# First keys loaded from ScalarE, five weight tiles from GpSimd, mask and coarse values in shared tile shapes

## The chip, the cores and the metric

The kernel runs on one core of one Trainium2 chip. Its time is the device time of one execution in microseconds (us). Besides the matmul engine TensorE (PE) it uses VectorE (DVE), ScalarE (ACT), GpSimd (POOL) and SyncE (SP), which before the change issues every transfer.

## What is computed

Local plus coarse attention over 2 batches, 8 heads, 576 positions and 64 channels, and then two expert layers, one behind the other, on 1152 tokens of 512 channels (2048 hidden):

```python
q_d, k_d, v_d = means of q, k, v over groups of 4 positions            # 144 coarse positions
out_up = repeat(softmax(q_d @ k_d.T / 8) @ v_d, 4)                      # coarse attention
scores = where(abs(i - j) < 4, q @ k.T / 8, -1e9)                       # local attention
attn = out_up + softmax(scores) @ v
x = attn.transpose(0, 2, 1, 3).reshape(1152, 512)
h = x @ w_in                                                            # first expert
x = ((a0 + a1 h + a2 h^2 + a3 h^3) / (1 + |b0||h| + |b1| h^2 + 1e-6)) @ w_out
h = x @ w_in2                                                           # second expert
out = (h * tanh(softplus(h))) @ w_out2
```

The weights are float64 in memory and are taken as pairs of 32-bit words.

## The kernel before

**Attention** is cut into 18 units of 128 query rows of a pair of heads: 16 that take four windows of one pair of heads, and two mixed ones that take the last window of all four pairs. A unit loads its queries (`qload`, L643) and the values of its windows (`vload`, L658), and goes through these steps on TensorE: `pe_a` turns the queries by transposes (L546); `pe_b` writes the band mask into the score bank by one matmul of the doubled identity `eye2` with `mask` (L702), adds the local scores (L709, 64 x 32 tiles) and the coarse scores (L717); `pe_d` turns the normalized weights (L786, L791); `pe_e` makes the coarse values (L816: for each half of the coarse positions and each head one product, 64 output channels) and the local values (L826). Between these steps VectorE and ScalarE do the softmax, GpSimd the normalization (L770, L775) and, for each pair of heads, the sums of values (L615, L619) that the coarse values read. `od_c` (L839) copies the coarse values out on ScalarE, and the results go as a high and a low half to `xh` and `xl`. Keys come once for each pair of heads and batch (`prep`, L554 and L558) and are turned on TensorE too.

**Experts.** The 32 weight tiles of 1 MB are loaded into two `raw` buffers (L983, L988), joined to f32 by ScalarE and VectorE (L1000 to L1031) and split into a high and a low half. The first expert's products are L1144 (in) and L1277 (out), the second's L1514 and, by a Strassen-like scheme of seven products, L1458 (in), and L1279 (out).

**The order** of every engine is made by a planner when the program is built (`Plan.run`): it takes each step's engines, estimated cost and priority and, engine by engine, starts the ready step with the lowest priority number. `UOFF` moves the priorities of the 18 units, `GOFF` those of the first weight tiles, `LOFF` those of the query loads; `SECOND`, `CLEAD` and `SUMS` are further numbers of this kind. Where the planner finds TensorE without a step in the first stretch, it writes a warm-up matmul into the program (L527, on the zero tile `blank`, into a spare bank). At run time each engine goes through its list in order, each instruction waiting for its operands alone; a transfer of SyncE waits besides for the eighth one before it.

Of the kernel before, what the change touches and what calls it, by code (L numbers as in the profile page):

```python
# [12 lines left out]
BF16 = mybir.dt.bfloat16  # L13
# [3 lines left out]
AF = mybir.ActivationFunctionType  # L17
ALU = mybir.AluOpType
AX = mybir.AxisListType

NEG = -1.0e9
# [15 lines left out]
SUMS = 5  # L37
# [3 lines left out]
UOFF = [-3.0, 0.0, 0.0, 3.0, 4.5, 3.0, 3.0, -1.5, 6.0, 0.0, 0.0, -4.5, -4.5, 4.5, 6.0, 4.5, -1.5, -1.5]  # L41
GOFF = [0.0, 0.0, 0.0, 0.0, -4.0, -4.0, -10.0, -6.0, 2.0, -4.0, 10.0, 12.0]
# [37 lines left out]
class Plan:  # L80
# [33 lines left out]
    def run(self, names):  # L114
# [3 lines left out]
        landed, moved = [0.0] * QUEUED, 0.0  # L118
# [75 lines left out]
        while True:  # L194
            for e in names:
# [3 lines left out]
                while ready[e]:  # L199
# [14 lines left out]
                    if e == "pool" or e == "dve" and t.port:  # L214

                        begin = max(now, port[0])
                        port[0] = begin + t.engs[e]
                    end = until[e] = begin + t.engs[e] * (2 if e == "pe" and now < COLD else 1)
                    there = end + LAT[e]
                    if t.dma:  # L220
                        end = begin
# [51 lines left out]
def kernel(  # L273
# [34 lines left out]
    eye2 = const.tile([128, 128], BF16, name="eye2")  # L308
    mask = const.tile([128, 11, WK], BF16, name="mask")
    band = const.tile([64, 92], BF16, name="band")  # L310
# [140 lines left out]
    def bands():  # L451
        nc.gpsimd.affine_select(
            out=band, in_=band, compare_op=ALU.is_ge, fill=NEG, base=-8, pattern=[[1, 92]], channel_multiplier=-1,
        )
        nc.gpsimd.affine_select(
            out=band, in_=band, compare_op=ALU.is_ge, fill=NEG, base=14, pattern=[[-1, 92]], channel_multiplier=1,
        )

    def masks(kind, w, n):
        for b in range(2):  # L460
            h = slice(HB * b, HB * b + HB)
# [10 lines left out]
    def eyes():  # L472
        for h in range(2):
            nc.vector.tensor_copy(out=eye2[:64, 64 * h:64 * h + 64], in_=ident[:64, :64])
# [11 lines left out]
    def under():  # L486
        nc.vector.memset(eye2[64:], 0.0)
        nc.vector.memset(mask[64:], 0.0)

    t_m = add({"dve": 0.1}, lambda: nc.vector.memset(band, 0.0), -1900)  # L490
    t_un = add({"dve": 0.4}, under, -880)
    t_cd = add({"dve": 0.6}, zeros, -1000)
    t_bn = add({"pool": 0.5}, bands, -900, after=[t_m])
    t_mk = [
        add({"dve": 0.2 + 0.05 * len(ws)}, lambda x=(i, ws): [masks(x[0], *w) for w in x[1]], (-890, MKP, MKP)[i], after=[t_bn])
# [42 lines left out]
    kv_done, unit_pe = {}, {}  # L538
# [9 lines left out]
    def prep(bb, p, prio, slots, start):  # L548
        kn = Buf(kn_s + (wide_s["kn"] if start else []))

        def load():
            src = k[bb, 2 * p:2 * p + 2]
            if start:
                nc.sync.dma_start(  # L554
# [8 lines left out]
        ld = add({"sp": 0.65}, load, prio - KOFF, take=[kn], chain="ld", dma=[(0.65, 1.59 if start else 1.84)])  # L563
# [65 lines left out]
    def unit(u, slots, start):  # L629
# [33 lines left out]
        vl = add({"sp": 1.0}, vload, prio + VOFF, take=[vw], chain="vw", dma=[(0.45, 0.11)] * 8 if mixed else [(0.45, 0.33)] * 4)  # L663
# [35 lines left out]
        def pe_b():  # L699

            hs = [slice(0, 64), slice(64, 128)]
            nc.tensor.matmul(  # L702
                sc.v[:, :nw * WK], eye2, mask[:, m0:m0 + nw].rearrange("p w x -> p (w x)"), start=True, stop=False,
            )
# [18 lines left out]
            {"pe": 1.6 if mixed else 0.86}, pe_b, prio,  # L723
            after=tq + [kv_done[p] for p in pairs] + [t_i16, t_un, t_mk[kind]],
# [83 lines left out]

        def pe_e():

            hs = [slice(0, 64), slice(64, 128)]
            for i, p in enumerate(pairs):
                m = 16 * nw // len(pairs)
                for t in range(2):
                    for hh, h in enumerate(hs):
                        nc.tensor.matmul(  # L816
                            po.v[h, m * i:m * i + m], vd[p][:, t, hh, :], pT.v[:72, 256 + 128 * t + 64 * hh + m * i:256 + 128 * t + 64 * hh + m * i + m],
                            start=(t == 0), stop=(t == 1),
                        )
            for m in range(2):  # L820
                for b in range(2):
                    for hh in range(2):
                        for a in range(2):
                            h, r = hs[hh ^ a], slice(64 * a, 64 * a + WK)
                            c = 128 * m + h.start + HB * b
# [748 lines left out]
```

## Time and profile before

| | us |
|---|---|
| median of 3 runs | 482.04 (481.93 to 483.39) |
| the profiled execution | 482.31 |
| its span in the profile | 480.4 |
| TensorE busy | 469.4 |
| VectorE busy | 377.0 |
| ScalarE busy | 338.3 |
| GpSimd busy, nearly all in the first 125 us | 57.1 |

A row of the profile gives the line of the kernel, the engine, the operation and the tiles that it writes and reads. TensorE's matmuls overlap one another, so that what one costs in the queue is the distance of its start from the next one's, and not its recorded duration. An f32 product is recorded as two passes, an f32 transpose as one. In the first 125 us attention, the first expert's products and the warm-up matmuls stand mixed in TensorE's list; behind it there are the experts alone.

### The profile page before, as it was taken

Reading aid. Unit: us, or ns where it says so; the run is one execution under the profiler, and the core shown is the slowest. Engines: PE = TensorE matmul, PEld = TensorE weight load, DVE = VectorE, ACT = ScalarE, POOL = GpSimd, SP = SyncE. Lnnn points to the kernel's source line nnn. Section 1 sums busy time; section 2 is a strip of 40 time slices with the busy share of each in tenths; the row PEclk is TensorE's granted clock in tenths of the full one; section 3 lists DMA queues with packets and bytes.
Section 4 is the critical chain, followed back from the end, with each engine's and each line's share of the span. In section 5 each row is a group of like instructions: output and inputs, shape, how many; then the busy total and the mean of one; then the engine's idle time right before and its main releaser. Section 6 shows DMA issues by size and latency. Waiting matters only on the chain.

```text
span 480.4 us, 9823 instructions
## 1 busy us (share of the span) xinstructions
PE 469.4 (98%) x4052; PEld 429.1 (89%) x4052; DVE 377.0 (78%) x565; ACT 338.3 (70%) x529; POOL 57.1 (12%) x80
## 2 busy tenths in 40 slices
PE   8998999999999999999999999999999999999996
PEld 4667888889999999999999999898989898989885
DVE  6677999899899968997998999988596669524342
ACT  5678898786889799998879797578666446422320
POOL 2644434563000000000000000000000000000000
PEclk9999999999999999999999999999999999999999
DMA  9878887611522312343022022134304220000103
GB/s 170 196 178 198 243 200 188 166 37 35 176 89 88 123 54 89 96 125 131 0 89 88 1 88 89 39 111 146 143 15 162 87 89 1 1 0 0 67 0 132
DMA packets 45981, 47.18 MB, mean 98 GB/s; under 512 B 30576, under 2 KB 31344, under 8 KB 45936
## 3 DMA queue, kind: packets, MB, share of 16 engines
q1 hardware_dynamic: 45936, 46.54, 33.7%
q8 instruction: 32, 0.52, 0.5%
q14 instruction: 13, 0.11, 0.1%
HBM read 44.17 MB, written 2.36 MB: 97 GB/s over the span
## 4 chain that ended last, share of the span: by engine, by line
PE 73%; DVE 13%; DMA 8%; ACT 3%; SPq 2%; issue 1%; ACTq 0%
PE psum L1279 19%; PE psum L1144 18%; PE psum L1277 15%; PE psum L1458 11%; PE psum L1514 5%; DMA att<-in_q_dram 3%; DMA raw<-in_moe_w_in_dram 3%; DVE wt L1014 1%; PE psum L826 1%; DMA att<-in_v_dram 1%; DVE xl L1300 1%; PE psum L546 1%; SPq L643 1%; DVE wrk L1318 1%; DVE wo L1031 1%
## 5 line engine op out<-in xcount | busy, mean ns | idle before, releaser
L1144 PE MATMUL psum<-xh,wi 128*128 128x384 f32 (+1 forms) x336 | 83.4, 319 | 0.2 <-DVE wrk L1173 0.2
L1277 PE MATMUL psum<-gg,wo 128*128 128x384 f32 (+1 forms) x480 | 76.3, 313 | 0.0
L1277 PEld LDWEIGHTS psum<-gg,wo 128*128 128x128 f32 x480 | 72.8, 189 | 0.4 <-issue 0.2
L1144 PEld LDWEIGHTS psum<-xh,wi 128*128 128x128 f32 x336 | 59.1, 189 | 1.4 <-issue 0.9
L1144 PE MATMUL psum<-xl,wi 128*128 128x384 f32 (+1 forms) x168 | 52.4, 312 | 0.0
L1279 PE MATMUL psum<-wo,gg 128*128 128x512 f32 x216 | 51.7, 391 | 0.0
L1279 PE MATMUL psum<-wo,late_g 128*128 128x512 f32 x216 | 51.3, 391 | 0.0
L1279 PEld LDWEIGHTS psum<-wo,late_g 128*128 128x128 f32 x216 | 40.4, 188 | 8.0
L1279 PEld LDWEIGHTS psum<-wo,gg 128*128 128x128 f32 x216 | 40.4, 188 | 7.9
L1014 DVE SCALAR_TENSOR_TENSOR wt<-wt,raw 128x1024 int32<-128x1024 int32 x32 | 40.0, 1252 | 6.8 <-ACT wt L1000 6.5
L1000 ACT ACTIVATE wt<-raw 128x1024 f32<-128x1024 f32 x32 | 36.5, 1140 | 10.9 <-DVE wo L1031 4.8
L1007 ACT ACTIVATE raw<-raw 128x1024 int32<-128x1024 uint16 x32 | 36.7, 1147 | 5.1 <-DMA raw<-in_moe_w_out_dram 3.4
L1514 PE MATMUL psum<-xh,wi 128*128 128x384 f32 x128 | 34.5, 335 | 0.0
L1144 PEld LDWEIGHTS psum<-xl,wi 128*128 128x128 f32 x168 | 31.8, 189 | 0.0
L1390 DVE TENSOR_TENSOR part<-psum,part 128x512 f32<-128x512 f32 x27 | 17.8, 687 | 13.7 <-PE psum L1279 13.7
L1144 PE MATMUL psum<-xh,late_r 128*128 128x384 f32 x96 | 25.5, 334 | 0.0
L527 PE MATMUL psum<-blank 128*128 128x480 bf16 x86 | 22.9, 390 | 1.2 <-DVE band L490 1.2
L1031 DVE TENSOR_TENSOR wo<-wt,wo 128x1024 fp32r<-128x1024 f32 x14 | 17.1, 1219 | 8.7 <-ACT wo L1026 8.7
L1026 ACT ACTIVATE wo<-wt 128x1024 fp32r<-128x1024 f32 x11 | 11.7, 1062 | 17.1 <-DVE wt L1020 7.7
L1514 PEld LDWEIGHTS psum<-xh,wi 128*128 128x128 f32 x128 | 23.3, 188 | 0.2
L1164 ACT ACTIVATE wrk<-psum 128x768 f32<-128x768 f32 (+1 forms) x27 | 19.8, 734 | 5.1 <-PE psum L1144 4.8
L1088 ACT ACT_TABLE_LOAD x17 | 21.8, 1283 | 0.3
(165 smaller groups left out, 1043.5 us busy)
## 6 DMA issues: line engine op xcount, KB each, us to landing
raw<-in_moe_w_in_dram SPq DMA_DIRECT2D x16, 1024.0 KB, 6.0
raw<-in_moe_w_out_dram SPq DMA_DIRECT2D x16, 1024.0 KB
att<-in_v_dram SPq DMA_DIRECT2D x64, 48.0 KB, 4.0
out_dram<-part SPq DMA_DIRECT2D x9, 256.0 KB, 2.1
att<-in_q_dram SPq DMA_DIRECT2D x16, 128.0 KB, 4.2
att<-in_k_dram SPq DMA_DIRECT2D x6, 288.0 KB, 4.5
att<-in_v_dram SPq DMA_DIRECT2D x6, 256.0 KB, 5.7
wrk<-in_k_dram SPq DMA_DIRECT2D x2, 288.0 KB
```

Of the source, the lines that this page charges most:

```text
L527: nc.tensor.matmul(view[:, :480], blank[:, :128], blank, start=True, stop=True)
L1000: nc.scalar.activation(out=t.v, in_=words(r)[:, :, 1].bitcast(F32), func=AF.Prelu if fold else AF.Identity, scale=2.0 ** -112, **({"alpha" ...
L1007: nc.scalar.activation(out=words(r)[:, :, 0], in_=r.v.bitcast(U16).rearrange("p (n four) -> p n four", four=4)[:, :, 1], func=AF.Copy, sca ...
L1014: nc.vector.scalar_tensor_tensor(out=ti, in0=ti, scalar=3, in1=words(r)[:, :, 0], op0=ALU.logical_shift_left, op1=ALU.bitwise_or)
L1031: ENG[e].tensor_tensor(out=w.v[:, 1], in0=s.v, in1=w.v[:, 0].bitcast(F32), op=ALU.subtract)
L1088: nc.scalar.preload_act_table_set(name)
L1144: nc.tensor.matmul(st.h.v[:, i, :T], w.v[:, ww, ks], xx[:, kk, c0:c0 + T], start=(nn == 0 and (st.big or i == 0)), stop=(nn == 3 * KD - 1 ...
L1164: nc.scalar.activation(out=vw(st.a), in_=H(), func=AF.Square)
L1277: nc.tensor.matmul(A(d)[:, :T], w.v[:, ww, lo + d * 128:lo + (d + 1) * 128], vw(gg)[:, i, :], start=start, stop=stop)
L1279: nc.tensor.matmul(A(d), vw(gg)[:, i, sl], w.v[:, ww, lo:lo + DM], start=start, stop=stop)
L1458: nc.tensor.matmul(dst.v[:, :TW], wv.v[:, ww, at:at + 128], x(h, kk), start=bool(take) and nn == 0, stop=nn == 5, skip_group_check=not take,)
L1514: nc.tensor.matmul(h.v[:, i, :TW], w.v[:, ww, at:at + 128], xx[:, kk, c0:c0 + TW], start=nn == 0, stop=nn == 3 * KD - 1)
```

## The change

- The keys of the second and third pair of heads are issued from ScalarE at its start; before, from SyncE.
- The first five weight tiles are issued from GpSimd, each placed behind a chosen unit's local values (`AFTER`); this is a place in the planned order, and no wait of the program.
- The mask is added by four matmuls on the 64 x 32 tiles of the local scores; `eye2`, `mask` and `band` hold both partition halves for it.
- The coarse values of both heads come from one full-width product for each half of the coarse positions, which also makes the two head pairings that nobody reads; `od_c` then picks the two useful blocks by two instructions.
- The planner's numbers change: `UOFF`, `GOFF`, `LOFF`, `SECOND`, `CLEAD`, `SUMS`, and the costs that it takes for `pe_b`, `pe_e`, `od_c` and the masks; its model of the transfers keeps a queue of eight for GpSimd apart.

```diff
-SECOND = 1.8
+SECOND = 1.2
-LEAD, CLEAD, LLEAD, OLAG = 38, 14, 40, 18
-PROL, PSTEP, VOFF, VROFF, LOFF, KOFF = -45, 2.5, 2, -1, 7, 9
+LEAD, CLEAD, LLEAD, OLAG = 38, 12, 40, 18
+PROL, PSTEP, VOFF, VROFF, LOFF, KOFF = -45, 2.5, 2, -1, 10, 9
-SUMS = 5
+SUMS = 0
+AFTER = [1, 3, 4, 5, 6]
+AHEAD = 2
-GOFF = [0.0, 0.0, 0.0, 0.0, -4.0, -4.0, -10.0, -6.0, 2.0, -4.0, 10.0, 12.0]
+GOFF = [0.0, 0.0, 0.0, 0.0, -4.0, -4.0, -20.0, -10.0, 8.0, 2.0, 0.0, 4.0]
...
     def masks(kind, w, n):
-        for b in range(2):
-            h = slice(HB * b, HB * b + HB)
+        for r0 in range(0, 128, HB):
+            b, h = r0 // HB % 2, slice(r0, r0 + HB)
...
+        ahead = start and 0 < p <= AHEAD
+
         def load():
             src = k[bb, 2 * p:2 * p + 2]
             if start:
-                nc.sync.dma_start(
+                (nc.scalar if ahead else nc.sync).dma_start(
...
-            nc.tensor.matmul(
-                sc.v[:, :nw * WK], eye2, mask[:, m0:m0 + nw].rearrange("p w x -> p (w x)"), start=True, stop=False,
-            )
+            for b in range(2):
+                for h in hs:
+                    r0 = h.start + HB * b
+                    nc.tensor.matmul(
+                        sc.v[r0:r0 + HB, :nw * WK], eye2[h, HB * b:HB * b + HB],
+                        mask[h, m0:m0 + nw].rearrange("p w x -> p (w x)"), start=True, stop=False, tile_position=(h.start, r0),
+                    )
...
-            {"pe": 1.6 if mixed else 0.86}, pe_b, prio,
+            {"pe": 1.52 if mixed else 0.78}, pe_b, prio,
...
                 for t in range(2):
-                    for hh, h in enumerate(hs):
-                        nc.tensor.matmul(
-                            po.v[h, m * i:m * i + m], vd[p][:, t, hh, :], pT.v[:72, 256 + 128 * t + 64 * hh + m * i:256 + 128 * t + 64 * hh + m * i + m],
-                            start=(t == 0), stop=(t == 1),
-                        )
+                    nc.tensor.matmul(
+                        po.v[:, 2 * m * i:2 * m * i + 2 * m], vd[p][:, t].rearrange("p h d -> p (h d)"),
+                        pT.v[:72, 256 + 128 * t:384 + 128 * t].rearrange("p (h x) -> p h x", h=2)[:, :, m * i:m * i + m],
+                        start=(t == 0), stop=(t == 1),
+                    )
...
-            {"pe": 1.75 if mixed else 0.98}, pe_e, prio, after=tp + [vl] + [vd_done[p] for p in pairs], take=[po, px, od, xt],
+            {"pe": 1.6 if mixed else 0.89}, pe_e, prio, after=tp + [vl] + [vd_done[p] for p in pairs], take=[po, px, od, xt],
...
         def od_c():
-            nc.scalar.activation(
-                out=od.v[:, :16 * nw], in_=po.v[:, :16 * nw], func=AF.Identity, scale=0.25
-            )
+            for hh in range(2):
+                h = slice(64 * hh, 64 * hh + 64)
+                nc.scalar.activation(
+                    out=od.v[h].rearrange("c (i x) -> c i x", x=m),
+                    in_=po.v[h, :128].rearrange("c (i h x) -> c i h x", h=2, x=m)[:, :, hh], func=AF.Identity, scale=0.25,
+                )
...
-        def load(g=g, r=r):
+        own = len(W) < len(AFTER)
+
+        def load(g=g, r=r, q=nc.gpsimd if own else nc.sync):
...
-        x = add({"sp": 0.5}, load, pr - LLEAD, take=[r], chain="wld", dma=[(0.5, 3.97)])
+        x = add({"pool" if own else "sp": 0.5}, load, pr - LLEAD, after=[v_loads[AFTER[len(W)]]] if own else [], take=[r],
+                chain="wld", dma=[(0.85 if own else 0.5, 3.97)])
```

TensorE's list holds 86 warm-up matmuls before and 112 now, 67 and 76 of them ahead of the first L1144; the matmuls of the experts are the same in number and size. SyncE's list at the program's start, before (L554 keys, L643 queries, L609 the values of a pair of heads, L658 the values of a unit's windows):

```order
L554 DMA att<-in_k_dram 96x2x384
L643 DMA att<-in_q_dram 128x4x64
L554 DMA att<-in_k_dram 96x2x384
L609 DMA att<-in_v_dram 64x2x512
L609 DMA att<-in_v_dram 8x2x512
L643 DMA att<-in_q_dram 128x4x64
L554 DMA wrk<-in_k_dram 96x2x384
L643 DMA att<-in_q_dram 128x4x64
L658 DMA att<-in_v_dram 48x4x64 x4
```

and now (the keys are L555, queries L645, values L611 and L660):

```order
L555 DMA att<-in_k_dram 96x2x384
L645 DMA att<-in_q_dram 128x4x64
L611 DMA att<-in_v_dram 64x2x512
L611 DMA att<-in_v_dram 8x2x512
L645 DMA att<-in_q_dram 128x4x64 x2
L660 DMA att<-in_v_dram 48x4x64 x4
```

Two of the three keys that stood in this list are gone from it; they now open ScalarE's list, ahead of its table load. GpSimd's list around the third unit, before (L615 and L619 sums of values, L870 the low half `xl`, L770 and L775 the normalization of a unit):

```order
L615 TENSOR_TENSOR wrk<-wrk 72x4x128
L619 TENSOR_TENSOR att<-wrk 72x2x2x64
L870 TENSOR_TENSOR xl<-att,xh 128x256
L770 TENSOR_TENSOR att<-att 128x4x48
L775 TENSOR_SCALAR att<-att 128x144
```

and now (L617, L621, L880, L776 and L781 in the same meaning, L995 the load of a weight tile):

```order
L617 TENSOR_TENSOR wrk<-wrk 72x4x128
L621 TENSOR_TENSOR att<-wrk 72x2x2x64
L995 DMA raw_74<-in_moe_w_in_dram 128x4x256
L617 TENSOR_TENSOR att<-att 72x4x128
L880 TENSOR_TENSOR xl<-att,xh 128x256
L776 TENSOR_TENSOR att<-att 128x4x48
L781 TENSOR_SCALAR att<-att 128x144
```

The first weight tile is issued here, and the normalization of the third unit now stands behind it and behind the fourth sum of values. TensorE's list at the first unit's scores and at its values, before:

```order
L702 LDWEIGHTS eye_62
L702 MATMUL psum<-mask,eye_62 128x192
L709 MATMUL psum<-att 32x48 x16
L717 MATMUL psum<-att 32x144 x4
...
L816 MATMUL psum<-att 64x64 x4
L826 MATMUL psum<-att 64x32 x16
```

and now (mask L707, local scores L715, coarse scores L723, coarse values L822, local values L833; the first two rows stand four times in a row):

```order
L707 LDWEIGHTS eye_62
L707 MATMUL psum<-mask,eye_62 32x192
...
L715 MATMUL psum<-att 32x48 x16
L723 MATMUL psum<-att 32x144 x4
...
L822 MATMUL psum<-att 128x128 x2
L833 MATMUL psum<-att 64x32 x16
```

The mask is cut into four tiles of 32 output rows, and four coarse products of 64 x 64 became two of 128 x 128; in the two mixed units 16 products of 64 x 16 became 8 of 128 x 32.

## Rows read from the trace of the kernel before

**Rows 1.** The page: busy us of each engine, share of the span, instructions.
```profile
PE 469.4 (98%) x4052; PEld 429.1 (89%) x4052; DVE 377.0 (78%) x565; ACT 338.3 (70%) x529; POOL 57.1 (12%) x80
```
**Rows 2.** Windows by stage: stretch and length, busy us by engine, clock, DMA share, GB/s.
```profile
0.00:33.00 33.00, 30.01 (x488) 18.46 (x489) 21.81 (x72) 21.22 (x56) 15.98 (x30) 1.00 0.90 194
...
125.00:260.00 135.00, 135.00 (x806) 135.00 (x805) 124.12 (x137) 119.39 (x137) 0.00 (x0) 1.00 0.27 90
260.00:310.00 50.00, 49.36 (x273) 47.39 (x272) 47.26 (x56) 38.78 (x47) 0.00 (x0) 1.00 0.12 43
```
**Rows 3.** Groups of the page (busy, mean ns), then TensorE's timeline (start, length).
```profile
L527 PE MATMUL psum<-blank 128*128 128x480 bf16 x86 | 22.9, 390 | 1.2 <-DVE band L490 1.2
...
29.39 1.78 PE L527 MATMUL psum<-blank 128*128 128x480 bf16 x8
31.01 0.38 PE L786 MATMUL psum<-ident,att 128*112 128x128 f32 x2
31.22 0.38 PE L791 MATMUL psum<-ident,att 128*72 128x128 f32 x2
```
**Rows 4.** TensorE's waits: for whom, us in total, times, longest.
```profile
PE psum L546 <- DMA att<-in_q_dram: 2.8, 3, 1.6
...
PE psum L816 <- POOL att L619: 1.1, 2, 0.7
PE psum L826 <- DMA att<-in_v_dram: 0.9, 2, 0.6
PE psum L1458 <- DVE wrk L1480: 0.6, 1, 0.6
```
**Rows 5.** TensorE's timeline at an unmixed unit, then at a mixed one.
```profile
34.48 0.28 PE L1144 MATMUL psum<-xh,wi 128*128 128x256 f32 x1
34.69 0.45 PE L816 MATMUL psum<-att 72*64 72x64 f32 x8
35.07 0.67 PE L826 MATMUL psum<-att 48*64 48x32 f32 x32
...
36.27 0.28 PE L1144 MATMUL psum<-xl,wi 128*128 128x256 f32 x1
36.39 0.28 PE L1144 MATMUL psum<-xh,wi 128*128 128x256 f32 x1
36.51 0.26 PE L702 MATMUL psum<-mask,eye 128*128 128x192 bf16 x1
36.70 0.54 PE L709 MATMUL psum<-att 64*32 64x48 f32 x32
...
64.77 1.11 PE L816 MATMUL psum<-att 72*64 72x16 f32 x32
65.81 0.67 PE L826 MATMUL psum<-att 48*64 48x32 f32 x32
```
**Rows 6.** Weight loads of 0 to 125 us by form: busy us, mean ns, idle before.
```profile
L1144 PEld LDWEIGHTS psum<-xh,wi 128*128 128x128 f32 x139 | 23.5, 190 | 1.4 <-issue 0.9 <-DVE wrk L1173 0.5
...
L816 PEld LDWEIGHTS psum<-att 72*64 72x64 f32 x192 | 7.1, 137 | 4.6 <-POOL att L619 1.6 <-issue 1.0 <-ACT att L801 0.6
...
L546 PEld LDWEIGHTS psum<-ident,att 128*128 128x128 f32 x36 | 4.2, 141 | 4.1 <-issue 1.8 <-DMA att<-in_q_dram 1.8
```
**Rows 7.** Chain that ended last (start, length), then SyncE's timeline.
```profile
17.15 2.02 SPq L983
19.27 6.06 DMA att<-in_q_dram
...
35.49 0.40 SPq L983 DMA_DIRECT2D raw<-in_moe_w_in_dram  x1
```
**Rows 8.** GpSimd's timeline: start, length, instruction, in brackets the idle time ahead of it.
```profile
28.20 1.31 POOL L615 TENSOR_TENSOR att<-att 72x512 f32<-72x512 f32 x1 [5.02 <-DMA att<-in_v_dram]
29.47 0.51 POOL L770 TENSOR_TENSOR att<-att 128x192 f32<-128x192 f32 x1
```
**Rows 9.** ScalarE's groups of 0 to 125 us: busy us, mean ns, idle before.
```profile
L839 ACT ACTIVATE att<-psum 128x64 f32<-128x64 f32 x18 | 4.0, 224 | 7.2 <-PE psum L826 7.0
```
**Rows 10.** SyncE's waits of 0 to 125 us: us in total, times, longest.
```profile
SPq L983 <- DVE wt L1014: 4.6, 1, 4.6
```

More of the change, by code (lines that the diff above doesn't have):

```diff
@@ L117, in run @@
         live, freed, port = {}, {}, [0.0]
-        landed, moved = [0.0] * QUEUED, 0.0
+        lanes, moved = {"sp": [0.0] * QUEUED, "pool": [0.0] * QUEUED}, 0.0
+        lanes["act"] = lanes["sp"]
         touched = {}
@@ L213, in run @@
                     begin = max(now, 0.65) if e == "sp" else now
-                    if e == "pool" or e == "dve" and t.port:
+                    if e == "pool" and not t.dma or e == "dve" and t.port:
                         begin = max(now, port[0])
@@ L220, in run @@
                     if t.dma:
-                        end = begin
+                        end, landed = max(begin, 0.65), lanes[e]
                         for issue, move in t.dma:
@@ L485 @@
     t_id = add({"pool": 1.1}, lambda: make_identity(nc, ident), -1000)
-    def under():
-        nc.vector.memset(eye2[64:], 0.0)
-        nc.vector.memset(mask[64:], 0.0)
     t_m = add({"dve": 0.1}, lambda: nc.vector.memset(band, 0.0), -1900)
-    t_un = add({"dve": 0.4}, under, -880)
     t_cd = add({"dve": 0.6}, zeros, -1000)
-    t_bn = add({"pool": 0.5}, bands, -900, after=[t_m])
+    t_bn = add({"pool": 1.0}, bands, -900, after=[t_m])
     t_mk = [
-        add({"dve": 0.2 + 0.05 * len(ws)}, lambda x=(i, ws): [masks(x[0], *w) for w in x[1]], (-890, MKP, MKP)[i], after=[t_bn])
+        add({"dve": 0.4 + 0.1 * len(ws)}, lambda x=(i, ws): [masks(x[0], *w) for w in x[1]], (-890, MKP, MKP)[i], after=[t_bn])
         for i, ws in enumerate((((0, 1), (1, 1), (2, 1), (3, 1)), ((4, 4),), ((8, 4),)))
@@ L561, in load @@
                 )
-        ld = add({"sp": 0.65}, load, prio - KOFF, take=[kn], chain="ld", dma=[(0.65, 1.59 if start else 1.84)])
+        ld = add({"act" if ahead else "sp": 0.65}, load, -2000 if ahead else prio - KOFF, take=[kn],
+                 chain=None if ahead else "ld", dma=[(0.65, 1.59 if start else 1.84)])
         copies = []
@@ L661, in vload @@
                     )
-        vl = add({"sp": 1.0}, vload, prio + VOFF, take=[vw], chain="vw", dma=[(0.45, 0.11)] * 8 if mixed else [(0.45, 0.33)] * 4)
+        vl = v_loads[len(v_loads)] = add({"sp": 1.0}, vload, prio + VOFF, take=[vw], chain="vw", dma=[(0.45, 0.11)] * 8 if mixed else [(0.45, 0.33)] * 4)
         def pe_a():
@@ L722, in unit @@
         tb = add(
-            {"pe": 1.6 if mixed else 0.86}, pe_b, prio,
-            after=tq + [kv_done[p] for p in pairs] + [t_i16, t_un, t_mk[kind]],
+            {"pe": 1.52 if mixed else 0.78}, pe_b, prio,
+            after=tq + [kv_done[p] for p in pairs] + [t_i16, t_mk[kind]],
             take=[sc, tm, s, pd],
@@ L807, in unit @@
         ]
+        m = 16 * nw // len(pairs)
         def pe_e():
@@ L838, in od_c @@
         def od_c():
-            nc.scalar.activation(
-                out=od.v[:, :16 * nw], in_=po.v[:, :16 * nw], func=AF.Identity, scale=0.25
-            )
-        to = add({"act": 0.11}, od_c, prio, after=[tf], use=[po, od])
+            for hh in range(2):
[3 more added lines that the diff above has]
+                    in_=po.v[h, :128].rearrange("c (i h x) -> c i h x", h=2, x=m)[:, :, hh], func=AF.Identity, scale=0.25,
+                )
+        to = add({"act": 0.21}, od_c, prio, after=[tf], use=[po, od])
         def xadd():
```

32 lines of the change are left out of this document (16 added, 16 removed).

## The prediction, written before the changed kernel ran

> **What bounds the kernel now.** I read the busy line first: TensorE is busy for 469.4 of 480.4 us, every other engine far less [rows 1]. The windows by stage say where the remainder lies: from 125 us to 260 us TensorE never stops, and around the change of experts it stands for 0.64 us in 50; the first 33 us hold 3 us of its idle time [rows 2]. The reader is to see a queue that is almost always full, so that the end moves by exactly what is put into that queue, taken out of it, or waited for in front of it. Some of what it holds is no work: the 86 warm-up matmuls on `blank` [rows 3]. Last I read TensorE's own waits [rows 4]: queries that have not landed (2.8 us in three waits), local values (0.9 us), the coarse values made by GpSimd (1.1 us), and 0.6 us at the first Strassen products.
>
> So I use a ledger: time = real matmuls + warm-up matmuls + waits + a head and a tail that the change leaves alone. It stands on one profiled execution of 482.31 us (span 480.4, 1.9 outside it), 0.27 us above the median of 482.04.
>
> **Warm-up matmuls.** They are written into the program by the planner, and run whether or not TensorE would have waited. The order has 86 before and 112 now: 67 and 76 of them ahead of the first expert matmul, 19 and 36 behind it. Eight in a row, from 29.39 to 31.01 us, take 1.62 us, so one is 0.20 us of queue [rows 3]. That adds 26 x 0.20 = **+5.2 us**. It costs nothing where it stands in place of a wait; the gain then shows in the term of the waits, which for the whole attention stage is at most 2.8 + 1.1 + 0.9 = 4.8 us [rows 4]. This bound is why I doubt a gain: the added filler is as large as all that waiting.
>
> **Mask in tile shapes, 18 units.** One full-array matmul of 192 columns becomes four on 64 x 32 tiles. Before, 0.19 us pass from the mask's start (36.51) to the first local score (36.70), although 256 columns in the full array take 0.12 us (36.27 to 36.39) [rows 5]. Some 0.10 us are therefore not the mask's columns but the change to tiles behind it. The same change shows where a full-array matmul is followed by the tiled coarse values: 0.21 us (34.48 to 34.69) in place of 0.12. The change now stands ahead of the mask instead of behind it. I take 0.02 us less each, **-0.4 us**. Bounds: the change of shape vanishes (18 x -0.10 = -1.8), or the two column tiles of a row half stream one after the other (another 192 columns, 0.08 by the 256-column row: +1.4). The Trainium skill ("TensorEngine Tiling (Array Packing)", Key Properties) says that a change of tiling mode drains TensorE; the rows agree, with 0.09 us, and by that rule the 0.10 us cannot be won by giving the mask its followers' shape, while a reading without it would book -1.8.
>
> **Coarse values in one shape.** Before, an unmixed unit has four products 72 x 64 with 64 columns, recorded as eight passes in 0.38 us (34.69 to 35.07), two column tiles side by side [rows 5]. Now two full-width products with 128 columns each compute all four head pairings, of which half are thrown away, in four passes. A full-array f32 pass with 128 columns takes 0.105 us (31.01 to 31.22 for two transposes) [rows 3]. Four are 0.42, and leaving for the 64 x 64 tiles of the local values costs 0.09 as above; entering from a full-array matmul saves 0.09. So 0.42 against 0.38: +0.04, and +0.13 where the work ahead is tiled, which I take for a third of the units: 16 x 0.07 = +1.1. In the two mixed units 16 products with 16 columns take 1.04 us (64.77 to 65.81); that is weight loading, 32 passes in pairs of 64 columns. Now there are 8 products, 16 passes, each with 128 weight columns. A load of 64 columns is recorded with 0.137 us, one of 128 with 0.190 (0.053 more per 64 columns, so 0.106 for 128), yet 0.141 for the transposes [rows 6]. At 0.106 they take 1.70, +0.66 each; at half, 0.85, -0.19 each. I take a value towards the upper row, since it is the one of plain products: 2 x 0.6 = +1.2. Together **+2.3 us**. Bounds: all passes at half (4 x 0.053 = 0.21 against 0.38, 16 x -0.17, with the mixed ones -3.1), or entry never saved and loads in full (16 x 0.13 + 2 x 0.75 = +3.6).
>
> **Loads.** Two keys leave SyncE for ScalarE and five weight tiles of 1 MB leave it for GpSimd. At 17.15 us SyncE spends 2.02 us on a weight issue, the query load behind it is issued at 19.27 and lands 6.06 us later, and TensorE waits for it [rows 7]. With the tile on another queue neither delay is in front of that query, and the query loads also come earlier in the order. I take 3.0 of the 3.7 us of waits for loads as gone: **-3.0 us**; bounds 0 and -3.7. ScalarE's two issues stand at its start, ahead of its table load, when TensorE runs warm-up matmuls; if that cover is gone they cost two issues, 0.8 us at the 0.40 us of the shortest issue in [rows 7].
>
> **GpSimd's queue.** No row of before shows a DMA issued there. An issue of the same tile costs SyncE 0.40 us, or 2.02 us when it is held up [rows 7]. Behind it in GpSimd's queue stand the sums of values, `xl`, and the normalization of the next unit, for which ScalarE, VectorE and then the transposes of TensorE wait. GpSimd is on the chain already: at 28.20 it had waited 5.02 us for a values load, with the normalization of a unit behind it [rows 8]. Five issues of about 1 us, most of it beside other work: **+0.6 us**, bounds -1.0 (that 5.02 us shortens) and +4.
>
> **Other work.** `od_c` becomes two ScalarE instructions of about 0.22 us [rows 9]: 18 x 0.22 = 4 us of ScalarE, beside TensorE, whose next products in the queue do not read that copy: 0 us, and 1 us if that cover is gone. Twelve more mask copies on VectorE and two selects on GpSimd lie ahead of the first scores, under warm-up matmuls: 0. In the second expert the order of Strassen sums, wide output products and first Strassen products changes: 36 wide output products now stand ahead of all Strassen products, where 0.6 us was waited [rows 4]. VectorE is busy for 47.26 of the 50 us there [rows 2], so I book 0 with bounds -0.6 and +2.
>
> **Sum.** 5.2 - 0.4 + 2.3 - 3.0 + 0.6 = +4.7 us. 482.31 + 4.7 = 487.0 against the profiled execution, **486.7** against the median, 1.0% slower.
>
> **Rivals.**
> *The cheap shapes win.* The full-width passes take half of what I say and the mask loses its change of shape: -3.1 - 1.8, and all waits go: 5.2 - 4.9 - 4.8 = -4.5, 477.5 us; with 3.0 of the waits gone 479.3. For it: a transpose's weight load of 128 columns is recorded with 0.141, not 0.190. Against it: transposes with 128 columns still pass at 0.105 us each. It decides if the coarse values take 0.25 us or less in an unmixed unit.
> *Nothing comes of it.* Coarse values at their old price, the mask half-way to its lower bound (-1.0), all load waits gone and GpSimd half-way to its own (-0.5): 5.2 - 1.0 - 3.7 - 0.5 = 0, 482 us.
> *The loads land no earlier.* All bytes move through the same engines; the tile still takes its share beside the query. Then the -3.0 falls away: 489.7. For it: in the first 33 us the engines are 0.90 busy [rows 2]. Against it: part of the delay was SyncE's own 2.02 us. The Trainium skill ("DMA: Bandwidth & Descriptors", Issuing engines are not separate DMA queues) says that DMAs started by any engine interleave on the same 16 engines and that issuing from several saves only the issue time; by that rule this rival would be the forecast, 489.7, and no run here has yet shown it.
> *GpSimd is held up.* SyncE once waited 4.6 us in front of a weight issue, until VectorE had joined the tile that held the buffer [rows 10]. If such a wait now stands in GpSimd's queue, a normalization waits behind it and TensorE with it: up to +4.6, 491.3 us.
>
> **How the numbers follow.** Forecast, 483.5 to 489: 0.45. Loads no earlier: 0.13. GpSimd held up: 0.15. Nothing: 0.14. Cheap shapes: 0.13. Three cases are slower: 0.73; 0.3% (1.4 us), about what a measurement of this kernel can tell from no change, leaves 0.14 for the same and 0.13 for faster. The range reaches down into the cheap shapes, 480.5, and up to the held GpSimd, 491.5, and leaves some 0.17 out.
>
> **What would show it.** The warm-up group at 112 instructions of 0.20 us in a row; an unmixed unit's coarse values near 0.42 us plus the change of shape, a mixed unit's near 1.7; the mask's start to the first local score near 0.09, with 0.21 in front of it; TensorE's waits for queries under 1 us. The forecast is wrong if the coarse values got cheaper, if the waits shrank by more than 4 us, or if TensorE waits for GpSimd's normalization by several us.

## The result, and the profile after

The changed kernel takes 486.74 us (486.17 to 488.83), 1.0104 times the kernel before (95% interval 1.0065 to 1.0143): 4.7 us slower, as forecast (486.7). Ratios here and below leave out the runs that took over 1.5% longer than the fastest of their kernel (one of twelve with five tiles from GpSimd, two of nine with mask and five tiles); medians count them. The profiled execution took 486.17 us, its span is 484.4 us. The page, with TensorE's busy time and matmuls, against [rows 1]:

```profile
PE 477.1 (99%) x4036; PEld 435.1 (90%) x4036; DVE 381.3 (79%) x576; ACT 343.7 (71%) x546; POOL 65.2 (13%) x87
...
L526 PE MATMUL psum<-blank 128*128 128x480 bf16 x112 | 29.6, 393 | 1.2 <-DVE band L490 1.2
```

TensorE is busy for 7.7 us more with 16 matmuls fewer; 6.7 us of this are recorded for the warm-up matmuls alone (22.9 before, [rows 3]). Windows by stage, columns as in [rows 2], first two of the kernel before, then the changed one:

```profile
33.00:48.00 15.00, 13.38 (x276) 11.20 (x278) 11.07 (x34) 12.92 (x32) 6.14 (x10) 1.00 0.71 167
48.00:125.00 77.00, 75.13 (x1394) 67.00 (x1393) 71.17 (x143) 61.51 (x147) 34.98 (x41) 1.00 0.61 156
```
```profile
0.00:33.00 33.00, 30.72 (x493) 18.79 (x493) 23.11 (x88) 21.12 (x59) 17.04 (x34) 1.00 0.82 179
33.00:48.00 15.00, 15.00 (x303) 11.78 (x305) 11.37 (x27) 12.29 (x34) 9.53 (x11) 1.00 1.03 228
48.00:125.00 77.00, 76.69 (x1316) 68.71 (x1309) 69.28 (x139) 64.72 (x155) 38.61 (x44) 1.00 0.48 130
125.00:260.00 135.00, 135.00 (x816) 135.00 (x815) 124.91 (x138) 119.57 (x138) 0.00 (x0) 1.00 0.28 95
260.00:310.00 50.00, 49.21 (x271) 47.13 (x270) 48.82 (x58) 40.28 (x47) 0.00 (x0) 1.00 0.18 63
```

In the first 125 us TensorE's idle time fell from 6.5 to 2.6 us, and from 33 to 48 us it no longer stands. Even so it has started 322 matmuls of the first expert by 125 us, and 352 before: 30 at 0.12 us [rows 5] are 3.6 of the 4.0 us between the two spans. Behind 125 us little changed (0.79 us stood around the change of experts, 0.64 before). So nearly all of the difference lies in the first 125 us. TensorE's waits, against [rows 4]:

```profile
PE psum L526 <- DVE band L490: 1.2, 1, 1.2
PE psum L545 <- ACT att L762: 0.8, 1, 0.8
...
PE psum L822 <- POOL att L621: 0.3, 1, 0.3
```

No wait for a load is left: of the 2.8 us for queries and 0.9 us for local values nothing, of the 1.1 us for the sums of GpSimd 0.3. TensorE's timeline, in the places of [rows 3, 5] (three unmixed units, then a mixed one, then a mask behind an expert matmul):

```profile
20.24 0.71 PE L822 MATMUL psum<-att 72*128 72x128 f32 x4
20.88 0.67 PE L833 MATMUL psum<-att 48*64 48x32 f32 x32
...
34.83 0.61 PE L822 MATMUL psum<-att 72*128 72x128 f32 x4
35.37 0.67 PE L833 MATMUL psum<-att 48*64 48x32 f32 x32
...
43.73 0.58 PE L526 MATMUL psum<-blank 128*128 128x480 bf16 x2
44.15 0.38 PE L792 MATMUL psum<-ident,att 128*112 128x128 f32 x2
...
44.58 1.78 PE L526 MATMUL psum<-blank 128*128 128x480 bf16 x8
46.20 0.61 PE L822 MATMUL psum<-att 72*128 72x128 f32 x4
46.74 0.67 PE L833 MATMUL psum<-att 48*64 48x32 f32 x32
47.34 0.26 PE L707 MATMUL psum<-mask,eye 64*32 64x192 bf16 x4
47.43 0.51 PE L715 MATMUL psum<-att 64*32 64x48 f32 x32
...
64.22 0.28 PE L1157 MATMUL psum<-xh,wi 128*128 128x256 f32 x1
64.34 1.87 PE L822 MATMUL psum<-att 72*128 72x32 f32 x16
66.14 0.67 PE L833 MATMUL psum<-att 48*64 48x32 f32 x32
...
67.46 0.29 PE L1157 MATMUL psum<-xh,wi 128*128 128x256 f32 x1
67.68 0.26 PE L707 MATMUL psum<-mask,eye 64*32 64x192 bf16 x4
```

Read by starts: the unmixed coarse values take 0.54 us behind full-array work (34.83 to 35.37; 0.38 before) and 0.64 behind the tiled coarse scores (20.24 to 20.88), the mixed ones 1.80 (64.34 to 66.14; 1.04 before), the mask 0.09 to its first local score (47.34 to 47.43; 0.19 before). Ten warm-up matmuls stand around the transposes, where [rows 5] has none. The first of the five issues on GpSimd, its timeline beside [rows 8]:

```profile
20.72 0.97 POOL L995 DMA_DIRECT2D raw<-in_moe_w_in_dram  x1
22.55 1.26 POOL L617 TENSOR_TENSOR att<-att 72x512 f32<-72x512 f32 x1 [0.86 <-DMA att<-in_v_dram]
```

An issue costs GpSimd 0.76 to 0.97 us and none waits for its buffer; GpSimd's 5.02 us in front of the sums became 0.86.

### The profile page after: what moved, and what is told of

Read it like the earlier page. It is cut to its first block, busy times and chain, and to the rows that moved or that the text cites. A ratio compares the mean times of both kernels' runs of the same rounds, so it can differ in the third digit from the quotient of the medians.

```text
span 484.4 us, 9858 instructions
## 1 busy us (share of the span) xinstructions
PE 477.1 (99%) x4036; PEld 435.1 (90%) x4036; DVE 381.3 (79%) x576; ACT 343.7 (71%) x546; POOL 65.2 (13%) x87
## 4 chain that ended last, share of the span: by engine, by line
PE 81%; DVE 11%; DMA 3%; ACT 2%; issue 1%; POOL 1%; SPq 0%; POOLq 0%; DVEq 0%
PE psum L1157 19%; PE psum L1292 18%; PE psum L1290 15%; PE psum L1471 11%; PE psum L1527 5%; PE psum L526 4%; PE psum L822 2%; PE psum L833 2%; DMA raw<-in_moe_w_in_dram 2%; PE psum L545 1%; DVE part L1380 1%; DVE xl L1313 1%; ACT att L589 1%; PE psum L723 1%; DVE wt L1026 1%; PE psum L715 1%
## 5 line engine op out<-in xcount | busy, mean ns | idle before, releaser
L526 PE MATMUL psum<-blank 128*128 128x480 bf16 x112 | 29.6, 393 | 1.2 <-DVE band L490 1.2
L1537 ACT ACTIVATE wrk<-psum 128x768 f32<-128x768 f32 x8 | 6.5, 814 | 24.5 <-PE psum L1527 24.5
```

What stands on the lines that cost most here:

```text
L526: nc.tensor.matmul(view[:, :480], blank[:, :128], blank, start=True, stop=True)
```

## The experiments

**How they add up.** Three groups of four kernels, each group on one chip, with runs of the kernel before between them (medians 481.1, 481.7 and 481.1 us). A kernel's median is compared within its group, the ratio across groups. Lines of an edited kernel are shifted by a few.

| kernel | us | ratio to before | 95% |
|---|---|---|---|
| changed, again | 487.02 | 1.0121 | 1.0097 to 1.0145 |
| changed, coarse values in old shapes | 483.64 | 1.0048 | 1.0030 to 1.0066 |
| changed, all loads from SyncE | 486.31 | 1.0118 | 1.0086 to 1.0151 |
| changed, last 36 warm-ups left out | 488.25 | 1.0141 | 1.0106 to 1.0177 |
| changed, 10 warm-ups left out | 486.19 | 1.0103 | 1.0079 to 1.0127 |
| changed order alone | 485.57 | 1.0088 | 1.0050 to 1.0127 |
| before, mask in tiles | 479.72 | 0.9965 | 0.9944 to 0.9986 |
| before, coarse values in new shape | 482.44 | 1.0009 | 0.9981 to 1.0037 |
| before, five tiles from GpSimd | 479.66 | 0.9961 | 0.9938 to 0.9983 |
| before, mask and five tiles | 478.78 | 0.9953 | 0.9923 to 0.9982 |
| the same, keys from ScalarE | 478.81 | 0.9979 | 0.9950 to 1.0009 |
| before, 5 more warm-ups | 480.32 | 0.9981 | 0.9961 to 1.0000 |

**The changed kernel again.**

> The changed kernel once more, unaltered, as the measure for the others of this group, which are all cut from it. Expected 486.7 us again, a ratio to the kernel before of 1.010 (1.0065 to 1.0143 so far).

487.02 us, 5.8 us above the kernel before by its ratio; it is the measure for the next three.

**Coarse values back in their old shapes**, with their one copy out, at their places in the changed order:

```diff
-                    nc.tensor.matmul(
-                        po.v[:, 2 * m * i:2 * m * i + 2 * m], vd[p][:, t].rearrange("p h d -> p (h d)"), ...
+                    for hh, h in enumerate(hs):
+                        nc.tensor.matmul(
+                            po.v[h, m * i:m * i + m], vd[p][:, t, hh, :], ...
```

> The changed kernel with the coarse values alone in their old shapes: for each head and half a product with 64 output channels, one copy out; every instruction stands at its place as before the edit. Ledger: the full-width products cost 16 x 0.06 us in unmixed units and 2 x 0.67 us in mixed ones by their starts in the two traces, so this version is 2.3 us faster than the changed kernel, 484.4 us (486.7 - 2.3). Rival, the shapes cost nothing because a later wait takes what they give: 486.7 us, and TensorE's waits in the attention stage grow by 2.3 us. Rival, full-width products are the cheaper ones: 487 us or more.

483.64 us, 3.4 less; the two intervals do not meet, so the new shape costs time here. TensorE's timeline of this version at an unmixed unit behind coarse scores and at a mixed unit:

```profile
19.71 0.45 PE L824 MATMUL psum<-att 72*64 72x64 f32 x8
20.10 0.67 PE L834 MATMUL psum<-att 48*64 48x32 f32 x32
...
63.32 0.28 PE L1155 MATMUL psum<-xh,wi 128*128 128x256 f32 x1
63.53 1.11 PE L824 MATMUL psum<-att 72*64 72x16 f32 x32
64.57 0.67 PE L834 MATMUL psum<-att 48*64 48x32 f32 x32
```

From the full-array matmul ahead to the local values it is 1.25 us (63.32 to 64.57), in the changed kernel 1.92 (64.22 to 66.14): 0.67 for one mixed unit. In 13 unmixed units the work ahead uses the full array, and they differ by 0.07 each (0.16 more for the coarse values, 0.09 less ahead of them). In three, coarse scores in tiles stand ahead; nothing is saved there, and they differ by 0.26 each (0.64 and 0.38). Together 2 x 0.67 + 13 x 0.07 + 3 x 0.26 = 3.0 of the 3.4 us; the rest is within the two intervals.

**All loads issued from SyncE again**, at their places in the changed order:

```diff
-                (nc.scalar if ahead else nc.sync).dma_start(
+                nc.sync.dma_start(
...
-        def load(g=g, r=r, q=nc.gpsimd if own else nc.sync):
+        def load(g=g, r=r, q=nc.sync):
```

> The changed kernel with the two keys and the five weight tiles issued from SyncE again, at the places in the planned order that they have in the changed kernel; TensorE, VectorE and the work of GpSimd keep their order. Theory that the other queues removed the waits for loads: TensorE's waits for queries and values come back, 3 to 4 us, and the time is 489.7 to 490.7 us. Rival, the planned order alone removed them, since all bytes move through the same 16 DMA engines: 486.7 us, with TensorE's waits as small as in the changed kernel (3.1 us in the listed rows). Third, the five issues on GpSimd cost it 0.76 to 0.97 us each and TensorE paid for it: 484 to 486 us.

486.31 us, no difference from 487.02. Its TensorE waits of the first 125 us:

```profile
...
PE psum L545 <- ACT att L762: 0.8, 1, 0.8
PE psum L545 <- ACT att L677: 0.4, 1, 0.4
```

No wait for queries or values, without the other queues. None of the seven profiles with the changed order has a wait for queries, whatever the queues; each of the four with the order before and all loads on SyncE has some (0.8 to 2.8 us). So in the changed kernel the planned order removed these waits, not the queues, and issuing from other engines was worth nothing that can be measured there (1.0118 against 1.0121). The Trainium skill ("DMA: Bandwidth & Descriptors", Issuing engines are not separate DMA queues) says that it saves only the time of the issue; this run agrees.

**The last 36 warm-up matmuls left out, then ten of them.** They are no part of the result. The first edit; the second has `if not 76 < len(warmed) <= 86`:

```diff
+        warmed.append(1)
+        if len(warmed) <= 76:
             nc.tensor.matmul(view[:, :480], blank[:, :128], blank, start=True, stop=True)
```

> The changed kernel without the last 36 of its 112 warm-up matmuls, those that stand behind the first expert matmul in TensorE's list; they are no part of the result. Ledger, each costs 0.20 us of a full queue: 36 x 0.20 = 7.2 us, 479.5 us. Rival, they stand in place of waits for work that is not ready: TensorE's waits grow by what they took, and the time stays at 486.7 us. Between the two the growth of the waits gives the share; with the clock of TensorE granted in full throughout in either case. If the granted clock falls below 1.00 in the first 125 us, a third cause is there and the time may rise above 486.7 us.

488.25 us: some 7.2 us of queue were taken out, and by the median none of it was gained. TensorE's timeline without the 36, and two windows (busy PE, PEld, DVE, ACT, POOL, then clock):

```profile
55.43 0.40 PE L796 MATMUL psum<-ident,att 128*112 128x128 f32 x2 [1.38 <-ACT att L593]
...
60.70 0.63 PE L1161 MATMUL psum<-xh,wi 128*128 128x256 f32 x2
61.13 0.41 PE L1161 MATMUL psum<-xl,wi 128*128 128x256 f32 x1
```
```profile
54.00:58.00 4.00, 2.62 (x52) 1.82 (x52) 3.25 (x7) 3.94 (x9) 2.11 (x3) 0.72 0.92 215
58.00:62.00 4.00, 4.00 (x47) 3.71 (x45) 3.56 (x7) 3.80 (x9) 0.00 (x0) 0.50 0.66 215
```

Where seven warm-up matmuls ran, TensorE now stands for 1.38 us, until ScalarE has made what the transposes read; then the granted clock falls to 0.50, the 1.2 GHz level, and the 256-column passes follow each other at 0.21 us (60.70 to 61.13 for two) in place of 0.12 [rows 5]. By the windows TensorE's idle time of the first 125 us is 6.9 us in place of 2.6, 4.3 more; the mean clock of this profile, 0.993 over 485 us, is 3.4 us of full clock that are missing. Together they are about what was taken out. So waits came back for more than half, and the clock took the rest: five of the six runs have a mean clock of 0.993 or less, and the sixth, at 1.00, took 485.19 us, 1.8 less than the changed kernel.

> The changed kernel without ten of its warm-up matmuls, those that run from 43.7 to 46.0 us, ahead of the waits that followed when all 36 later ones were left out; warm-up matmuls are no part of the result. If the ten are pure cost: 10 x 0.20 = 2.0 us less than the changed kernel, 485.0 us, 1.008 of the kernel before. If they stand in place of waits: TensorE waits there instead, 487.0 us, and if the standing is long enough the granted clock falls below 1.00 behind it and the time rises to 488 us or more.

486.19 us: 0.9 less by the ratios, between the two answers, and the interval meets that of the changed kernel. The clock held (0.998 or more in all six runs). TensorE's timeline without the ten, to be read against 43.73 to 47.43 of the changed kernel above:

```profile
43.57 0.38 PE L796 MATMUL psum<-ident,att 128*112 128x128 f32 x2
...
44.37 0.71 PE L826 MATMUL psum<-att 72*128 72x128 f32 x4 [0.20 <-DVE att L860]
...
46.05 0.26 PE L711 MATMUL psum<-mask,eye 64*32 64x192 bf16 x4 [0.30 <-ACT att L758]
```

The transposes start 0.58 us earlier, the coarse values 1.83, the mask only 1.29: the work behind the removed matmuls was not ready, and waits for VectorE (0.20) and ScalarE (0.30, and 0.8 a little later) stand in their place.

**The changed order alone**: coarse values and loads undone as above and the mask too, so that only the planner's numbers and costs (and the copies for the second half of the mask) are the new ones.

```diff
-            for b in range(2):
-                for h in hs: ...
+            nc.tensor.matmul(
+                sc.v[:, :nw * WK], eye2, mask[:, m0:m0 + nw].rearrange("p w x -> p (w x)"), start=True, stop=False,
+            )
```

> The changed kernel with its three other parts undone at once: coarse values in their old shapes, the mask as one full-array matmul, keys and weight tiles issued from SyncE. What is left of the change is the planned order with its 26 more warm-up matmuls. Theory that the shapes and the order share the cost and the queues are worth nothing: undoing the coarse values gave -3.4 us and undoing the queues -0.7 us, of which the latter is no more than scatter; 487.0 - 3.4 + 0.3 for the mask = 483.9 us, 1.005 to 1.006 of the kernel before. Rival, the order itself is neutral, since its warm-up matmuls stand where TensorE would have waited (+5.2 and -4.2 us by the two traces): the kernel before plus 1.0, 482 us, 1.002 or less.

1.0088, 4.2 us above the kernel before, 2.4 at the least: the order costs time by itself, and the rival (neutral order) fell. The theory's 1.005 to 1.006 lies at the lower edge of the interval. By the ratios the order is the largest part of the loss; with 2.4 to 6.1 against 3.4 for the coarse values that rank is not shown. This version is also 0.0040 above the one with only the coarse values undone, so mask and queues seem to give 1.9 us in the changed order; the two intervals overlap. The one profile is of the longest of the seven runs (490.21 us, mean clock 0.993). It shows where that run stood, and a window behind the longer stand:

```profile
PE psum L820 <- POOL att L621: 2.5, 1, 2.5
PE psum L545 <- ACT att L758: 1.7, 1, 1.7
```
```profile
90.00:92.00 2.00, 2.00 (x39) 1.94 (x38) 0.00 (x0) 0.78 (x4) 0.81 (x2) 0.50 0.42 117
```

The fallen clock is part of that run's time. The five runs with a mean clock of 0.998 or more took 484.9 us in the mean, the 16 such runs of the kernel before 481.0, so the order's cost is there without it.

**The mask alone in tiles, in the order before.**

```diff
-                sc.v[:, :nw * WK], eye2, mask[:, m0:m0 + nw].rearrange("p w x -> p (w x)"), start=True, stop=False,
+            for b in range(2):
+                for h in hs: ...
+                        sc.v[r0:r0 + HB, :nw * WK], eye2[h, HB * b:HB * b + HB], ...
```

> The kernel before with the mask alone in the 64 x 32 tile shape, everything else in its order. By the trace of the changed kernel the change of shape only moves ahead of the mask: -0.02 us in each of 18 units, -0.3 to -0.4 us, 480.7 us (ratio 0.999). Rival, the change of shape vanishes: -1.8 us, ratio 0.996. Rival, the copies for the second half of the mask delay VectorE at the start: +0.5 to +1 us, ratio 1.001 to 1.002.

0.9965: faster by 1.7 us (0.7 to 2.7), more than the 0.4 that the starts give. Its profile has these waits for queries, and SyncE's first weight issue:

```profile
PE psum L546 <- DMA att<-in_q_dram: 0.8, 2, 0.5
```
```profile
16.55 0.41 SPq L987 DMA_DIRECT2D raw<-in_moe_w_in_dram  x1
```

TensorE waits 0.8 us for queries here, 2.8 in the profile of before, where this issue took 2.02 us [rows 7]. It takes no new mask for that: with five more warm-up matmuls and the mask of before (last experiment) the same issue took 0.40 us and the queries 1.0 us, with the new coarse values 0.64 and 2.0. The profile of before shows an execution with long waits. Part of the gain is the clock: the mean clock was 0.996 or less in 1 of 11 runs, against 13 of 29 of the kernel before beside it. Runs with 0.998 or more took 479.8 and 481.0 us in the mean, which leaves 1.2. Where that comes from was not settled.

**The coarse values alone in the new shape, in the order before** (the first diff reversed, with its two copies out).

> The kernel before with the coarse values alone in the new shape (two full-width products of which half is thrown away, two copies out), everything else in its order. Ledger by the starts in the traces: 16 x 0.07 + 2 x 0.66 = +2.4 us, 483.5 us, ratio 1.005. By what undoing it in the changed kernel gave: +3.4 us, 484.5 us, ratio 1.007. Rival, in this order the shape is hidden by waits that follow it: ratio 1.000 to 1.002.

1.0009, +0.4 us, at most 1.8: less than the starts give (2.4 in the expectation). TensorE's timeline in the profile of this version, taken from the second longest of twelve runs (484.96 us), and its windows:

```profile
43.61 0.41 PE L546 MATMUL psum<-ident,att 128*128 128x128 f32 x2 [1.84 <-DMA att<-in_q_dram]
```
```profile
42.00:44.00 2.00, 0.39 (x4) 0.42 (x5) 0.12 (x1) 2.00 (x4) 0.97 (x2) 1.00 0.58 105
44.00:46.00 2.00, 2.00 (x13) 1.94 (x12) 1.91 (x4) 0.64 (x4) 0.00 (x0) 0.59 0.47 106
```

In the order before there is a place where TensorE waits for a query (1.62 us in the profile of before, 1.84 here, 0.51 with the mask in tiles). What a unit costs more ahead of such a place could be taken from the wait; the longer wait here does not show it, so this is argued and not shown. And here the clock falls behind the wait (0.59, then 0.55 from 46 to 48 us), as in the experiment without warm-up matmuls.

**Five weight tiles from GpSimd, in the order before.**

```diff
-        def load(g=g, r=r):
+        def load(g=g, r=r, q=nc.gpsimd if len(W) < 5 else nc.sync):
...
-                nc.sync.dma_start(
+                q.dma_start(
```

> The kernel before with the first five weight tiles issued from GpSimd, at the places in the planned order that they had on SyncE. In this order TensorE waits 2.8 us for queries, one of which stands in SyncE's list behind a weight issue of 2.02 us. Theory that the queue is what held the query: these waits fall under 1 us and the time by 1 to 3 us, 478 to 480 us. Rival, as undoing the queues in the changed kernel suggests, the place in the order and the bytes decide: the waits stay and the time is 481 us. Third, an issue on GpSimd that waits for its buffer holds up the normalization: up to +4.6 us, 486 us.

0.9961: 1.9 us faster (0.8 to 3.0). Its TensorE waits of the first 125 us:

```profile
PE psum L791 <- POOL att L775: 1.1, 2, 0.9
PE psum L546 <- ACT att L675: 0.9, 1, 0.9
...
```

No query is waited for, against 0.8 to 2.8 us in the four profiles with this order and all loads on SyncE; GpSimd's normalization is, for 1.1 us, 0.9 of it in one unit. So the mechanism of the prediction's load term exists, in the order for which it was worked out, and is worth nothing that shows in the other. How much of the 1.9 us it is stays open: the 2.02 us of [rows 7] are one execution's, and runs with a mean clock of 0.998 or more took 479.5 against 481.0 us, 1.5 less.

**Both on the kernel before, then the keys as well.** The first joins the last two edits of the kernel before; the second adds

```diff
-                nc.sync.dma_start(
+                (nc.scalar if 0 < p <= 2 else nc.sync).dma_start(
```

> The kernel before with two parts of the change that each gained in its order: the mask in the 64 x 32 tile shape (ratio 0.9965 alone) and the first five weight tiles issued from GpSimd (0.9961 alone). If the gains are of separate causes they add: 0.9965 x 0.9961 = 0.9926, 478.1 us against 481.7 us. Rival, both gain by the same thing, the waits for queries in the first 125 us, which are there to lose only once (2.8 us in the trace of before): 0.996, 479.7 us.

> The same two parts on the kernel before, and the keys of the second and third pair of heads issued from ScalarE as well, so that SyncE's list at the start holds the queries earlier. If the keys' issues hold up the first queries, up to 0.8 us less than with the two parts (two issues of 0.40 us): ratio 0.991. Rival, they lie under warm-up matmuls and the bytes decide: the same ratio as with the two parts.

0.9953 (0.9923 to 0.9982) and 0.9979, medians 478.78 and 478.81: the interval holds both the 0.9926 of gains that add and the 0.996 of the rival, so this run does not decide between them. The runs with a mean clock of 0.998 or more lean to adding: 478.2 us in five of them against 480.7 of the kernel before, 2.6 less, where the two parts alone had 1.2 and 1.5. The keys' place makes no difference that these intervals show. The first of the two beats both kernels: by the medians 2.3 us against the kernel before and, by the ratios, 7 to 8 against the changed one. But the clock is less steady: in four of its nine runs the mean is 0.996 or less, and two of these took 485 us. TensorE's timeline in its profile, and a window behind it:

```profile
61.86 0.41 PE L795 MATMUL psum<-ident,att 128*72 128x128 f32 x2 [0.37 <-POOL att L779]
```
```profile
66.00:68.00 2.00, 2.00 (x12) 1.84 (x12) 1.52 (x5) 1.18 (x2) 0.69 (x2) 0.57 1.08 273
```

**Five more warm-up matmuls ahead of the query's wait, in the order before.**

```diff
+        warmed.append(1)
+        for i in range(6 if len(warmed) == 70 else 1):
             nc.tensor.matmul(view[:, :480], blank[:, :128], blank, start=True, stop=True)
```

> The kernel before with five more warm-up matmuls (1.0 us) at 39.9 us, ahead of the place at 41.7 us where TensorE waits 1.6 to 1.8 us for a query. In the kernel before with the new coarse shapes this wait was followed by 3.3 us at half the granted clock (0.55 to 0.59), and about half of the runs of the kernel before have a mean clock of 0.993 to 0.996. If the standing brings the clock down: the wait becomes 0.6 to 0.8 us, the mean clock is 0.998 or more in nearly all runs, and the median is 0 to 1 us lower, ratio 0.998 to 1.000. Rival, the warm-up matmuls only delay what stands behind them: +1.0 us, ratio 1.002, with the clock as scattered as before.

0.9981 (0.9961 to 1.0000), 0.8 us less by the medians. TensorE's timeline and a window:

```profile
42.13 0.41 PE L550 MATMUL psum<-ident,att 128*128 128x128 f32 x2 [0.66 <-DMA att<-in_q_dram]
```
```profile
44.00:46.00 2.00, 2.00 (x36) 1.80 (x35) 0.96 (x5) 2.00 (x6) 0.87 (x2) 1.00 0.87 178
```

1.0 us more in the queue cost nothing; the rival (+1.0, 1.002) falls. That the wait behind it took it up is argued: it is 0.66 us here and 1.62 in the profile of before, but 0.51 with the mask in tiles, where nothing was put ahead of it. The mean granted clock was 0.996 or less in 2 of 12 runs, against 10 of 26 of the kernel before beside it: in the expected direction, and too few to call it shown.

## Why the prediction came out right, step by step

**The ledger held; two of its terms hold for other reasons than it gave, and that the sum met the first result to a tenth is luck.** The same kernel again was 5.8 us slower (4.7 to 7.0), and the runs split this into other parts: +4.2 for the order, +3.5 for the coarse values, -1.9 for mask and queues together (by the ratios; the last is not clear of noise).
- *The bound* (TensorE's queue) held: 3.6 of the 4.0 us between the spans lie in the first 125 us, and from 125 to 260 us TensorE never stands in either kernel.
- *Warm-up matmuls, +5.2.* The count and the 0.20 us are right; that they are a cost is for the most part not. Leaving ten out (2.0 us) gave 0.9, leaving 36 out (7.2 us) gave nothing by the median and 1.8 in the one run whose clock held. They are rather a gauge: the new order leaves TensorE without ready work for longer, and the planner writes that time into the list. As the price of the order they served: order alone +4.2 us (2.4 to 6.1) against the +2.8 that the prediction had for warm-up matmuls, loads and GpSimd together.
- *Coarse values, +2.3.* The mechanism is right and the size too small. The starts give 3.0: 0.07 in an unmixed unit and 0.67 in a mixed one, against 0.07 and 0.60 in the forecast, but 0.26 in place of 0.13 where the work ahead is tiled. Undoing them gave 3.4; in the order before the same edit costs 0.4 (1.8 at most), for a reason that stays open. The rival of cheap shapes asked for 0.25 us in an unmixed unit; it is 0.54.
- *Mask, -0.4.* The step is right by the rows: the local scores follow 0.09 us behind the mask, and from the expert matmul ahead to the mask it is 0.22 us (67.46 to 67.68 in the changed kernel) in place of 0.12. The change of shape moved and did not vanish; only in the five units where the mask stands right behind the local values (46.74 to 47.34, 0.60 as from 35.07 to 35.67 in the order before) there is none ahead of it. Together -0.3. The Trainium skill ("TensorEngine Tiling (Array Packing)", Key Properties) says that changing the tiling mode drains TensorE; these rows agree, with 0.09 to 0.10 us. The run gave more than the step, 1.7 us, in part by the clock.
- *Loads, -3.0.* The waits went (3.7 to 0), but not by the queues: with everything on SyncE they are gone too. "With the tile on another queue neither delay is in front of that query" fits the order before (-1.9 us) and is false as the cause here. And the 3.7 us, as the 2.02 us of the issue, are those of the one execution that the ledger stood on. Three other profiles with SyncE's list as before (mask in tiles, new coarse values, five more warm-up matmuls) have 1.0 to 2.0 us of waits for loads and 0.40 to 0.64 us for that issue. So the term fits that profile and is too large for these, which have about half of its waits or less. The rival "loads land no earlier" was right about the queues and wrong about its time, since the order removed the waits by itself.
- *GpSimd, +0.6.* Five issues of 0.76 to 0.97 us, no wait for a buffer, 0.3 us of TensorE's wait: the rival "held up" did not happen. *Sums of the second expert*: 0, within 0.15 us. *Copies of `od_c`*: no wait of TensorE for them is listed.

The sum by the rows of the two traces is 5.2 + 3.0 - 0.3 - 3.9 (idle time of the first 125 us) = +4.0 us, and 4.0 us lie between the spans. The prediction's own sign of being wrong, waits that shrink by more than 4 us, stands right at the edge (3.9 by the windows, 4.2 by the listed waits). The match is closer than such sums can be, for about a microsecond of waits moves from run to run: the changed kernel's second profile has a span of 485.6 us, with 0.7 us of waiting for values that the first does not have.

## What to carry to other kernels

A warm-up or filler instruction that a planner writes into a full queue is first a sign that nothing is ready there: what it costs is found by leaving it out, and not by its length. A gain from another issue queue belongs to the order it was worked out in; where a new order removes the same wait, it cannot be had twice. Waits of one profiled execution are not those of the kernel: three profiles of near relatives had about half of them or less. Parts that gain (mask and GpSimd's issues, 0.9953 together) can be buried under parts that lose (the coarse shape, the new order), so each is to be timed on the old plan first.

## What the hardware showed

The granted clock of TensorE fell from 2.4 to 1.2 GHz behind stands of very different length: 2.5 us (order alone, then 0.50), 1.84 us (then 0.59 and 0.55 over 4 us), 1.38 us in a stretch with further waits (0.50 in 58 to 62 us), and 0.37 us with mask and five tiles (0.57 in 66 to 68 us), where no stand over 0.1 us lies in the 40 us ahead of that one. In the profile of before it stayed at 1.00 behind 1.62 us:

```profile
44.00:46.00 2.00, 2.00 (x19) 2.00 (x18) 1.81 (x5) 1.51 (x7) 0.00 (x0) 1.00 0.66 152
```

So the length of one stand does not tell whether the clock falls; what else decides was not tested. The mean clock of a run shows it: of the fourteen profiles, the four with a mean of 0.996 or less have such a stretch at 1.2 GHz in the first 125 us, and the other ten run at 1.2 GHz only in their last 4 us.

The mean clock of the kernel before was 0.996 or less in 32 of the 72 runs beside the experiments, and these took 482.0 us in the mean, the others 480.9. That of the changed kernel was so in none of 12. Without its 36 later warm-up matmuls it was 0.993 or less in 5 of 6, without ten of them 0.998 or more in all 6. So these warm-up matmuls also keep the clock up, though the order alone, which has them all, fell to 0.996 or less in 2 of 7. No term of the prediction had this.
